# The backward products of a windowed attention in two blocks of four, and one of them in two PSUM tiles

## The chip, the cores and the metric

The kernel runs on one NeuronCore of a Trainium2 chip. The metric is the device time of one execution in microseconds (us), median of several runs. The instructions of the five engines appear here as PE (TensorE matmuls; PEld are its weight loads), ACT (ScalarE), DVE (VectorE), POOL (GpSimd) and SP (SyncE); the last two mainly issue DMAs.

## The reference

The reference computes attention inside 8 x 8 windows of a 256 x 256 picture with 384 channels, in bf16, and all its gradients:

```python
def _fwd_reference(x, wqkv, wo):
    # x: (1, 256, 256, 384) -> xw: (1024 windows, 64 tokens, 384)
    qkv = xw @ wqkv
    q, k, v = qkv[..., :C], qkv[..., C:2 * C], qkv[..., 2 * C:]
    p = softmax(einsum('bqc,bkc->bqk', q, k) * C ** -0.5)
    o = einsum('bqk,bkc->bqc', p, v) @ wo
    return o   # windows put back in their places

def reference(x, wqkv, wo, grad_out):
    out, vjp = jax.vjp(_fwd_reference, x, wqkv, wo)
    return (out, *vjp(grad_out))   # out, dx, dwqkv, dwo
```

## The kernel before, in words

**Tiles.** A tile is two windows, one above the other in the picture: 128 tokens on 128 partitions, the first window on partitions 0 to 63 (`LO`), the second on 64 to 127 (`HI`). Four tiles (`QT`) make a quad, and 128 quads (`NQ`) make the picture. Everything is done quad by quad.

**Weights folded ahead.** Products of weights alone are formed once (`A1_sb`, `A2_sb`, `A3_sb`, `Bm_sb`), so that a quad needs fewer matmuls.

**The front of a quad** prepares it:
- `front_transpose`: DMA transposes, issued on SP, of x and of the output's gradient (`do`) into `xdT`.
- `front_project` (phase "yg"): 18 matmuls of 512 columns with whole 128 x 128 weights, six outputs of three matmuls each, in `ps_yg`; copied to `ygT` in bf16, and transposed by three DMAs into `yg`.
- `front_scores`: the scores of the attention and their counterpart of the gradient into `ps_S`, the one tile of pool `psS` (one PSUM bank).
- `front_softmax`, `front_exp`, `front_ds`: softmax on DVE with one exponential on ACT. They leave `pds`: p and dS.
- `front_zb` (phase "zb"), four times: 6 matmuls of 384 columns, copied by ACT.

**The back of a quad** uses it. `back_transpose` transposes p and dS inside each window on DVE (`pdsT`). Then come products of p, dS or their transposes with 384 columns: W (p with do), U (dS with x), out, and dx (three terms summed in PSUM). Each is formed in two pairs of tiles, p = 0 and p = 1; so there are eight product pairs. In `pair`, each window is a 64 x 64 matmul, and four of them, on the four quarters of the array, start within 0.01 us of each other; the text calls these four a group. W, U and out take one group per pair, dx three. `out` and `dx` are copied to `stage` tiles and stored by three DMAs each on POOL (`back_out`); W and U stay on the chip in `W_sb` and `U_sb` (`back_uw`, L273 to L279).

**Weight gradients.** `weight_grad` (phase "dw") is a generator: each step issues one matmul (128 x 128 weights, 384 columns) that sums x with U or W of the six quads before into `ps_dw`, the one tile of pool `psW`. There are six such chains, and each quad runs one: 24 matmuls from quad 6 on, fewer before. The loop places these matmuls between other work with `fill(chain, n)`. After its last matmul DVE adds `ps_dw` to an accumulator (`G_acc`, `F_acc`; L310, L312).

**Order.** It is written out by hand for PE, ACT, DVE, POOL and SP: every engine works in the order in which the program issues. In an iteration of the main loop (L345 to L374): the do loads of the quad four ahead, the DMA transposes of the quad two ahead, the back's transposes of quad b, the projection of quad b + 1, x loads, then W of both pairs, half of the chain's matmuls, U of both pairs, out of pair 0, the rest of the chain, out of pair 1, dx of both pairs, and the scores and zb phase of quad b + 1.

**PSUM.** Pool `psT` has three tiles of two banks each. ps_yg, ps_W, ps_U, ps_out, ps_dx and ps_zb all take theirs from it in turn, so a product's first matmul waits until the tile that was given out three before it has been copied. `psS` and `psW` have a bank each.

Of the kernel before, what the change touches and what calls it, by code (L numbers as in the profile page):

```python
# [9 lines left out]
ALU = mybir.AluOpType  # L10
AX = mybir.AxisListType
BF16 = mybir.dt.bfloat16
F32 = mybir.dt.float32
ENG = mybir.EngineType

P = 128
# [4 lines left out]
QT = 4  # L21
# [4 lines left out]
def kernel(  # L26
# [11 lines left out]
    nc = tc.nc  # L38
    B, H, W, C = x.shape
# [10 lines left out]
    SPAN = NCH  # L50
# [3 lines left out]
    uwp = ctx.enter_context(tc.tile_pool(name="uwp", bufs=SPAN + 1))  # L54
# [3 lines left out]
    psT = ctx.enter_context(tc.tile_pool(name="psT", bufs=3, space=bass.MemoryType.PSUM))  # L58
    psS = ctx.enter_context(tc.tile_pool(name="psS", bufs=1, space=bass.MemoryType.PSUM))
    psW = ctx.enter_context(tc.tile_pool(name="psW", bufs=1, space=bass.MemoryType.PSUM))  # L60

    mm = nc.tensor.matmul
# [35 lines left out]
    def cut(i):  # L98
        return slice(i * P, (i + 1) * P)
# [9 lines left out]
    def dram(ap, q, t):  # L109
        band, qb = divmod(q, QPB)  # L110
        c0 = (qb * QT + t) * WIN
        return ap[0, band * 2 * WIN:(band + 1) * 2 * WIN, c0:c0 + WIN, :]

    def dram_half(ap, q, t, h):
        band, qb = divmod(q, QPB)
        c0 = (qb * QT + t) * WIN
        r0 = (band * 2 + h) * WIN
        return ap[0, r0:r0 + WIN, c0:c0 + WIN, :]

    st = [dict() for _ in range(NQ)]  # L120
    vec, act = nc.vector.tensor_copy, nc.scalar.copy

    def load_x(q, eng):
        st[q]["x"] = x_tok = tokp.tile([P, QT, C], BF16, name="x_tok")
        for t in range(QT):
            eng.dma_start(out=x_tok[:, t, :], in_=dram(x, q, t))

    def load_do(q):
        st[q]["do"] = do_tok = tokp.tile([P, QT, C], BF16, name="do_tok", bufs=5)
        for t in range(QT):  # L130
            nc.gpsimd.dma_start(out=do_tok[:, t, :], in_=dram(grad_out, q, t))  # L131
# [21 lines left out]
    def swap_halves(q):  # L153
        s = st[q]
        s["xs"] = x_sw = tokp.tile([P, QT // 2, C], BF16, name="x_sw", bufs=SPAN + 1)
        for o, i in ((LO, HI), (HI, LO)):
            nc.vector.tensor_copy(out=x_sw[o], in_=s["x"][i, 1:QT:2, :])
# [3 lines left out]
    def front_project(q):  # L161
        s = st[q]
        s["ygT"] = ygT = quad.tile([P, 2 * CK, QT * P], BF16, name="ygT")
        s["yg"] = yg = quad.tile([P, 2 * CK, QT, P], BF16, name="yg")
        for js, copy in (((0, 1), act), ((2, 3), act), ((4,), act), ((5,), vec)):
            ps = psT.tile([P, 2, QT * P], F32, tag="t", name="ps_yg")
            for i, aj in enumerate(js):
                a, j = divmod(aj, CK)
                A_sb = A3_sb if a else A2_sb
                for m in range(CK):  # L170
                    mm(ps[:, i], lhsT=A_sb[:, m, cut(j)], rhs=s["xdT"][:, a, :, m, :],  # L171
                       start=(m == 0), stop=(m == CK - 1))
            copy(out=ygT[:, js[0]:js[0] + len(js), :], in_=ps[:, 0:len(js)])  # L173
            if js[-1] % 2:
                ks = slice(js[-1] - 1, js[-1] + 1)
                nc.sync.dma_start_transpose(yg[:, ks].rearrange("p j t k -> p (j t) k"),
                                            ygT[:, ks].rearrange("p j k -> p (j k)"))
# [71 lines left out]

    def pair(ps, p, terms):
        t0, t1 = 2 * p, 2 * p + 1
        n = len(terms)
        for k, (lt, rt) in enumerate(terms):
            for o, b, i, t in ((LO, 0, LO, t0), (HI, 0, HI, t0), (HI, 1, LO, t1), (LO, 1, HI, t1)):
                mm(ps[o, b, 0:C], lhsT=lt[i, t, :], rhs=rt(i, t), start=(k == 0), stop=(k == n - 1))  # L257

    def terms_of(q):
        s = st[q]  # L260
        yg = s["yg"]
        p_, ds = s["pds"][:, 0], s["pds"][:, 1]
        pT, dsT = s["pdsT"][:, 0], s["pdsT"][:, 1]
        return {
            "W": [(p_, lambda i, t: s["do"][i, t, :])],
            "U": [(dsT, lambda i, t: s["x"][i, t, :])],
            "out": [(pT, lambda i, t: s["zb"][i, t, 1, :])],
            "dx": [(ds, lambda i, t: yg[i, 0:CK, t, :]),
                   (p_, lambda i, t: yg[i, CK:2 * CK, t, :]),
                   (dsT, lambda i, t: s["zb"][i, t, 0, :])],  # L270
        }

    def back_uw(q, which, p, copy):  # L273
        s = st[q]
        if p == 0:
            s[which] = uwp.tile([P, QT, C], BF16, name=which + "_sb")
        ps = psT.tile([P, 2, 512], F32, tag="t", name="ps_" + which)
        pair(ps, p, terms_of(q)[which])
        copy(out=s[which][:, 2 * p:2 * p + 2, :], in_=ps[:, :, 0:C])  # L279

    def back_out(q, which, p, copy, dst):
        ps = psT.tile([P, 2, 512], F32, tag="t", name="ps_" + which)
        pair(ps, p, terms_of(q)[which])
        o = stage.tile([P, 2, C], BF16, name=which + "_sb")
        copy(out=o[:], in_=ps[:, :, 0:C])  # L285
        nc.gpsimd.dma_start(out=dram(dst, q, 2 * p), in_=o[:, 0, :])  # L286
        nc.gpsimd.dma_start(out=dram_half(dst, q, 2 * p + 1, 1), in_=o[LO, 1, :])  # L287
        nc.gpsimd.dma_start(out=dram_half(dst, q, 2 * p + 1, 0), in_=o[HI, 1, :])  # L288
# [5 lines left out]
    def weight_grad(c, upto, pool, tag):  # L294
        which, acc = (("U", G_acc), ("W", F_acc))[c // CK]
        ma = c % CK
        first = covered[c] == 0
        todo = [(q, t) for q in range(covered[c], upto) for t in range(QT)]
        covered[c] = upto
        if not todo:  # L300
            return
        ps = pool.tile([P, C], F32, tag=tag, name="ps_dw")
        for k, (q, t) in enumerate(todo):
            s = st[q]
            xt = s["xs"][:, t // 2, :] if t % 2 else s["x"][:, t, :]
            mm(ps[:], lhsT=xt[:, cut(ma)], rhs=s[which][:, t, :],  # L306
               start=(k == 0), stop=(k == len(todo) - 1))
            if k == len(todo) - 1:
                if first:
                    nc.vector.tensor_copy(out=acc[:, ma, :], in_=ps[:])  # L310
                else:
                    nc.vector.tensor_tensor(out=acc[:, ma, :], in0=ps[:], in1=acc[:, ma, :], op=ALU.add)  # L312
            yield

    def fill(chain, n):
        for _ in range(n):
            if next(chain, 0) == 0:
                return
# [12 lines left out]
    with tc.manual_schedule(engines={ENG.PE, ENG.Activation, ENG.DVE, ENG.Pool, ENG.SP}):  # L331
        load_x(0, nc.gpsimd)
        load_do(0)
        load_x(1, nc.gpsimd)
        load_do(1)
        front_transpose(0)
        front_transpose(1)
        for q in (2, 3):
            load_x(q, nc.gpsimd)
            load_do(q)  # L340
        front_project(0)
        front_scores(0)
        front_softmax(0)
        zb_phase(0, 1)
        for b in range(NQ):  # L345
            f = b + 1
            ahead = f < NQ
            if b + 4 < NQ:
                load_do(b + 4)
            if b + 2 < NQ:  # L350
                front_transpose(b + 2)
            back_transpose(b)
            if ahead:
                front_project(f)
            if b + 4 < NQ:
                load_x(b + 4, nc.sync)
            chain = weight_grad(b % NCH, b, psW, "w")
            half = 2 * QT * min(b, SPAN) // 4
            back_uw(b, "W", 0, act)
            back_uw(b, "W", 1, vec)  # L360
            swap_halves(b)
            fill(chain, half)
            back_uw(b, "U", 0, act)
            back_uw(b, "U", 1, vec)
            back_out(b, "out", 0, act, out_0)
            for _ in chain:
                pass
            back_out(b, "out", 1, act, out_0)
            back_out(b, "dx", 0, vec, out_1)
            back_out(b, "dx", 1, act, out_1)  # L370
            if ahead:
                front_scores(f)
                front_softmax(f)
                zb_phase(f, f + 1 if f + 1 < NQ else None)  # L374
        for c in sorted(range(NCH), key=lambda c: covered[c]):
            for _ in weight_grad(c, NQ, psT, "t"):
                pass
# [59 lines left out]
```

## Time and profile before

| | |
|---|---|
| median of 3 runs (lowest to highest) | 2013.76 us (2013.29 to 2017.31) |
| the profiled execution, its span | 2016.49 us, 2014.7 us |
| TensorE busy | 1993.8 us (99%), granted clock 0.998 |
| VectorE, ScalarE, GpSimd busy | 69%, 63%, 56% |
| one quad, from quad 6 on | 15.40 us |

The profile is that of one execution. A line of its groups gives line, engine, operation, what is written and read, and the count, then the busy time in us, the mean duration in ns, and the idle time before the instructions with what ended it. A line of the timeline gives start and duration in us, then the instructions; those that follow each other closely are merged (x8), and PEld stands beside PE. A line of the windows gives a stretch, its length, the busy time (and count) of PE, PEld, DVE, ACT and POOL, the granted clock, the DMAs' share and GB/s. Starts of single instructions are given in us from the start of the span; where one quad is followed, the leading 1000 is left out after the first mention (12.362 is 1012.362).

### The profile page before, as it was taken

Reading aid. Unit: us, or ns where it says so; the run is one execution under the profiler, and the core shown is the slowest. Engines: PE = TensorE matmul, PEld = TensorE weight load, DVE = VectorE, ACT = ScalarE, POOL = GpSimd, SP = SyncE. Lnnn points to the kernel's source line nnn. Section 1 sums busy time; section 2 is a strip of 40 time slices with the busy share of each in tenths; the row PEclk is TensorE's granted clock in tenths of the full one; section 3 lists DMA queues with packets and bytes.
Section 4 is the critical chain, followed back from the end, with each engine's and each line's share of the span. In section 5 each row is a group of like instructions: output and inputs, shape, how many; then the busy total and the mean of one; then the engine's idle time right before and its main releaser. Section 6 shows DMA issues by size and latency. Waiting matters only on the chain.

```text
span 2014.7 us, 52710 instructions
## 1 busy us (share of the span) xinstructions
PE 1993.8 (99%) x20862; PEld 1074.6 (53%) x20862; DVE 1394.9 (69%) x2713; ACT 1268.9 (63%) x1689; POOL 1132.0 (56%) x2070
## 2 busy tenths in 40 slices
PE   7999999999999999999999999999999999999998
PEld 4555555555555555555555555555555555555554
DVE  4776677667766776776677667766766776677664
ACT  5666666666666666666666666666666666666663
POOL 5565565555555555655555565555555555555552
PEclk9999999999999999999999999999999999999999
DMA  9999999999999999999999999999999999999982
GB/s 206 213 222 214 208 207 203 202 208 210 196 214 210 199 202 213 210 203 214 199 202 214 193 220 205 199 203 216 207 197 213 206 200 214 207 204 208 206 178 73
DMA packets 979287, 408.89 MB, mean 203 GB/s; under 512 B 864352, under 2 KB 953440, under 8 KB 979040
## 3 DMA queue, kind: packets, MB, share of 16 engines
q1 hardware_dynamic: 879568, 252.26, 75.8%
q0 software_dynamic: 99072, 152.96, 31.2%
q8 instruction: 164, 2.69, 0.6%
q14 instruction: 83, 0.68, 0.1%
q10 hardware_dynamic: 400, 0.29, 0.0%
HBM read 101.84 MB, written 101.84 MB: 101 GB/s over the span
## 4 chain that ended last, share of the span: by engine, by line
PE 97%; DMA 2%; DVE 1%; issue 0%; ACT 0%; SPq 0%; POOL 0%; POOLq 0%
PE ps_dw L306 26%; PE ps_zb L232 25%; PE ps_yg L171 24%; PE ps_dx L257 6%; PE ps_S L187 6%; PE ps_W L257 4%; PE ps_out L257 3%; PE ps_U L257 3%; DMA xdT<-do_tok 1%; DMA yg<-ygT 1%; DMA x_tok<-in_x_dram 0%; PE ps_e L396 0%; ACT dwo_sb L397 0%; DVE ygT L173 0%; DVE pdsT L247 0%
## 5 line engine op out<-in xcount | busy, mean ns | idle before, releaser
L286 POOL DMA_DIRECT2D out_dram<-out_sb x256 | 139.8, 546 | 721.4 <-ACT out_sb L285 715.3
L234 ACT CAST zb<-ps_zb 128x768 bf16<-128x768 f32 x512 | 408.1, 797 | 189.7 <-PE ps_zb L232 171.1
L171 PE MATMUL ps_yg<-xdT,A_sb 128*128 128x512 bf16 x2304 | 518.5, 379 | 0.9 <-DMA xdT<-do_tok 0.9
L232 PEld LDWEIGHTS <-xdT 128*128 128x128 bf16 x3072 | 290.0, 98 | 187.4
L173 ACT CAST ygT<-ps_yg 128x1024 bf16<-128x1024 f32 (+1 forms) x384 | 321.6, 872 | 101.2 <-PE ps_yg L171 100.7
L171 PEld LDWEIGHTS <-A_sb 128*128 128x128 bf16 x2304 | 225.4, 98 | 259.4 <-issue 1.4
L232 PE MATMUL ps_zb<-A_sb,xdT 128*128 128x384 bf16 x1536 | 334.6, 327 | 0.0
L232 PE MATMUL ps_zb<-Bm_sb,xdT 128*128 128x384 bf16 x1536 | 333.3, 326 | 0.0
L285 ACT CAST out_sb<-ps_out 128x768 bf16<-128x768 f32 x256 | 205.1, 802 | 150.5 <-issue 143.3
L131 POOL DMA_DIRECT2D do_tok<-in_grad_out_dram x512 | 272.9, 542 | 33.8 <-issue 16.0
L279 ACT CAST U_sb<-ps_U 128x768 bf16<-128x768 f32 x128 | 102.3, 799 | 238.0 <-PE ps_U L257 238.0
L306 PE MATMUL ps_dw<-U_sb,x_tok 128*128 128x384 bf16 x768 | 251.0, 328 | 0.0
L306 PE MATMUL ps_dw<-W_sb,x_tok 128*128 128x384 bf16 x768 | 251.0, 328 | 0.0
L306 PE MATMUL ps_dw<-W_sb,x_sw 128*128 128x384 bf16 x768 | 249.7, 326 | 0.0
L306 PE MATMUL ps_dw<-U_sb,x_sw 128*128 128x384 bf16 x768 | 249.7, 326 | 0.0
L247 DVE STREAM_TRANSPOSE pdsT<-pds 32x256 bf16<-32x256 bf16 x512 | 223.2, 436 | 12.0
L306 PEld LDWEIGHTS <-x_tok 128*128 128x128 bf16 x1536 | 149.6, 97 | 143.8 <-issue 60.8
L306 PEld LDWEIGHTS <-x_sw 128*128 128x128 bf16 x1536 | 150.4, 98 | 82.8
L279 DVE CAST U_sb<-ps_U 128x768 bf16<-128x768 f32 x128 | 122.6, 958 | 97.3 <-PE ps_U L257 97.0
L209 DVE TENSOR_REDUCE rs<-e 128x4 f32<-128x256 f32 x128 | 53.8, 420 | 171.4 <-ACT e L203 171.4
L288 POOL DMA_DIRECT2D out_dram<-dx_sb x256 | 144.7, 565 | 30.5 <-DMA out_dram<-out_sb 23.9
L287 POOL DMA_DIRECT2D out_dram<-dx_sb x256 | 144.7, 565 | 27.9 <-DMA out_dram<-out_sb 20.2
(71 smaller groups left out, 2606.3 us busy)
## 6 DMA issues: line engine op xcount, KB each, us to landing
do_tok<-in_grad_out_dram POOLq DMA_DIRECT2D x512, 96.0 KB, 5.0
x_tok<-in_x_dram SPq DMA_DIRECT2D x496, 96.0 KB, 4.1
out_dram<-out_sb POOLq DMA_DIRECT2D x256, 96.0 KB, 4.0
out_dram<-out_sb POOLq DMA_DIRECT2D x512, 48.0 KB, 4.2
out_dram<-dx_sb POOLq DMA_DIRECT2D x256, 96.0 KB, 3.6
out_dram<-dx_sb POOLq DMA_DIRECT2D x512, 48.0 KB, 3.7
yg<-ygT SPq DMA_TRANSPOSE x384, 5.2
xdT<-x_tok SPq DMA_TRANSPOSE x128, 5.9
```

Source lines behind the costliest of these rows:

```text
L131: nc.gpsimd.dma_start(out=do_tok[:, t, :], in_=dram(grad_out, q, t))
L171: mm(ps[:, i], lhsT=A_sb[:, m, cut(j)], rhs=s["xdT"][:, a, :, m, :], start=(m == 0), stop=(m == CK - 1))
L173: copy(out=ygT[:, js[0]:js[0] + len(js), :], in_=ps[:, 0:len(js)])
L232: mm(ps[:, i, 0:C], lhsT=s["xdT"][:, 0, t, m, :], rhs=w[:, m, :], start=(m == 0), stop=(m == CK - 1))
L234: nc.scalar.copy(out=s["zb"][:, t], in_=ps[:, :, 0:C])
L247: nc.vector.transpose(out=dst[h + 32 * c:h + 32 * c + 32, :, r, :], in_=src[h + 32 * r:h + 32 * r + 32, :, c, :])
L257: mm(ps[o, b, 0:C], lhsT=lt[i, t, :], rhs=rt(i, t), start=(k == 0), stop=(k == n - 1))
L279: copy(out=s[which][:, 2 * p:2 * p + 2, :], in_=ps[:, :, 0:C])
L285: copy(out=o[:], in_=ps[:, :, 0:C])
L287: nc.gpsimd.dma_start(out=dram_half(dst, q, 2 * p + 1, 1), in_=o[LO, 1, :])
L288: nc.gpsimd.dma_start(out=dram_half(dst, q, 2 * p + 1, 0), in_=o[HI, 1, :])
L306: mm(ps[:], lhsT=xt[:, cut(ma)], rhs=s[which][:, t, :], start=(k == 0), stop=(k == len(todo) - 1))
```

## The change

- The eight product pairs are issued in two blocks, one for each pair: W, U, dx, out. A quarter of the chain's matmuls stand before the first block and the rest before the second. `swap_halves` follows the first block.
- W of a pair takes two PSUM tiles of one bank each in use: its first tile of the pair goes to `ps_We` in pool `psS` (the scores' bank) and is copied by ACT; the second goes to one bank of a `psT` tile and is copied by DVE. Each copy has 384 columns.
- U is copied by ACT in both pairs (before: ACT, DVE), dx by DVE in both (before: DVE, ACT), out by ACT as before.
- The projection's six outputs are copied as 1, 1, 2, 2, all by ACT (before: 2, 2, 1 by ACT and 1 by DVE).
- The accumulation of a chain is issued when the chain is run to its end, which is behind W of the second pair.

```diff
-        for js, copy in (((0, 1), act), ((2, 3), act), ((4,), act), ((5,), vec)):
+        for js, copy in (((0,), act), ((1,), act), ((2, 3), act), ((4, 5), act)):
...
-    def pair(ps, p, terms):
+    def pair(banks, p, terms):
...
-                mm(ps[o, b, 0:C], lhsT=lt[i, t, :], rhs=rt(i, t), start=(k == 0), stop=(k == n - 1))
+                mm(banks[b][o], lhsT=lt[i, t, :], rhs=rt(i, t), start=(k == 0), stop=(k == n - 1))
...
-    def back_uw(q, which, p, copy):
+    def two_banks(name):
+        ps = psT.tile([P, 2, 512], F32, tag="t", name=name)
+        return ps, (ps[:, 0, 0:C], ps[:, 1, 0:C])
+
+    def back_w(q, p):
         s = st[q]
         if p == 0:
-            s[which] = uwp.tile([P, QT, C], BF16, name=which + "_sb")
-        ps = psT.tile([P, 2, 512], F32, tag="t", name="ps_" + which)
-        pair(ps, p, terms_of(q)[which])
-        copy(out=s[which][:, 2 * p:2 * p + 2, :], in_=ps[:, :, 0:C])
+            s["W"] = uwp.tile([P, QT, C], BF16, name="W_sb")
+        one = psS.tile([P, C], F32, tag="s", name="ps_We")
+        _, two = two_banks("ps_W")
+        pair((one[:], two[0]), p, terms_of(q)["W"])
+        act(out=s["W"][:, 2 * p, :], in_=one[:])
+        vec(out=s["W"][:, 2 * p + 1, :], in_=two[0])
+
+    def back_u(q, p):
+        s = st[q]
+        if p == 0:
+            s["U"] = uwp.tile([P, QT, C], BF16, name="U_sb")
+        ps, banks = two_banks("ps_U")
+        pair(banks, p, terms_of(q)["U"])
+        act(out=s["U"][:, 2 * p:2 * p + 2, :], in_=ps[:, :, 0:C])
...
-            half = 2 * QT * min(b, SPAN) // 4
-            back_uw(b, "W", 0, act)
-            back_uw(b, "W", 1, vec)
-            swap_halves(b)
-            fill(chain, half)
-            back_uw(b, "U", 0, act)
-            back_uw(b, "U", 1, vec)
-            back_out(b, "out", 0, act, out_0)
-            for _ in chain:
-                pass
-            back_out(b, "out", 1, act, out_0)
-            back_out(b, "dx", 0, vec, out_1)
-            back_out(b, "dx", 1, act, out_1)
+            left = QT * min(b, SPAN)
+            for p, n in ((0, left // 4), (1, left - left // 4)):
+                fill(chain, n)
+                back_w(b, p)
+                if p == 1:
+                    for _ in chain:
+                        pass
+                back_u(b, p)
+                back_out(b, "dx", p, vec, out_1)
+                back_out(b, "out", p, act, out_0)
+                if p == 0:
+                    swap_halves(b)
```

In `weight_grad` the accumulation moves from the last step of the loop to behind the loop. The numbers of matmuls, of weight loads and of DVE instructions stay as they are; ACT has one copy more a quad.

More of the change, by code (lines that the diff above doesn't have):

```diff
@@ L271, in terms_of @@
         }
-    def back_uw(q, which, p, copy):
+    def two_banks(name):
+        ps = psT.tile([P, 2, 512], F32, tag="t", name=name)
+        return ps, (ps[:, 0, 0:C], ps[:, 1, 0:C])
+    def back_w(q, p):
         s = st[q]
         if p == 0:
-            s[which] = uwp.tile([P, QT, C], BF16, name=which + "_sb")
-        ps = psT.tile([P, 2, 512], F32, tag="t", name="ps_" + which)
-        pair(ps, p, terms_of(q)[which])
-        copy(out=s[which][:, 2 * p:2 * p + 2, :], in_=ps[:, :, 0:C])
+            s["W"] = uwp.tile([P, QT, C], BF16, name="W_sb")
[11 more added lines that the diff above has]
+        act(out=s["U"][:, 2 * p:2 * p + 2, :], in_=ps[:, :, 0:C])
     def back_out(q, which, p, copy, dst):
-        ps = psT.tile([P, 2, 512], F32, tag="t", name="ps_" + which)
-        pair(ps, p, terms_of(q)[which])
+        ps, banks = two_banks("ps_" + which)
+        pair(banks, p, terms_of(q)[which])
         o = stage.tile([P, 2, C], BF16, name=which + "_sb")
@@ L307, in weight_grad @@
                start=(k == 0), stop=(k == len(todo) - 1))
[L308 to L312, printed above, removed]
             yield
+        if first:
+            nc.vector.tensor_copy(out=acc[:, ma, :], in_=ps[:])
+        else:
+            nc.vector.tensor_tensor(out=acc[:, ma, :], in0=ps[:], in1=acc[:, ma, :], op=ALU.add)
     def fill(chain, n):
```

## The prediction

> **What bounds the kernel now.** The page comes first: busy shares, then the chain that ended last.
>
> ```profile
> PE 1993.8 (99%) x20862; PEld 1074.6 (53%) x20862; DVE 1394.9 (69%) x2713; ACT 1268.9 (63%) x1689; POOL 1132.0 (56%) x2070
> ...
> PE 97%; DMA 2%; DVE 1%; issue 0%; ACT 0%; SPq 0%; POOL 0%; POOLq 0%
> ```
>
> TensorE's own order sets the end. But "busy" lasts from a matmul's start to its modelled end (0.33 us for 384 columns, issued every 0.163), so short waits hide inside it. I therefore read starts of single instructions in the trace. The quad period, from one first ps_S matmul to the next, is 15.40 us for all 121 periods from quad 6 on (110.44 to 1974.38 us). One quad in the timeline, first around ps_W:
>
> ```profile
> 1012.39 0.59 ACT L173 CAST ygT<-ps_yg 128x512 bf16<-128x512 f32 x1
> ...
> 1013.04 0.11 PEld L257 LDWEIGHTS <-pds 64*64 64x64 bf16 x3 [0.23 <-issue]
> 1013.08 0.80 ACT L279 CAST W_sb<-ps_W 128x768 bf16<-128x768 f32 x1
> ...
> 1013.32 0.34 PE L306 MATMUL ps_dw<-W_sb,x_tok 128*128 128x384 bf16 x1
> ```
>
> The second W pair waits for a PSUM tile: ACT's 512-column ygT copy ends at 12.983 and the matmul starts at 13.034, 0.362 after the first pair's start, where 0.187 is usual. Then the switches between 64x64 and 128x128 work:
>
> ```profile
> 1014.96 0.33 PE L306 MATMUL ps_dw<-W_sb,x_tok 128*128 128x384 bf16 x1
> 1015.12 0.33 PE L306 MATMUL ps_dw<-W_sb,x_sw 128*128 128x384 bf16 x1
> ...
> 1015.38 0.52 PE L257 MATMUL ps_U<-x_tok,pdsT 64*64 64x384 bf16 x8
> 1015.73 0.33 PE L257 MATMUL ps_out<-zb,pdsT 64*64 64x384 bf16 x4
> ...
> 1015.99 0.34 PE L306 MATMUL ps_dw<-W_sb,x_tok 128*128 128x384 bf16 x1
> ```
>
> ps_dw to ps_dw is 0.163, ps_dw to ps_U 0.256: a switch in costs 0.093, and the first group of four after it 0.024 more (0.187 to the next group, then 0.163). Leaving, ps_out's group to ps_dw is 0.265 and the next spacing 0.172: 0.112. Last, the copies by form:
>
> ```profile
> L173 ACT CAST ygT<-ps_yg 128x1024 bf16<-128x1024 f32 x256 | 259.1, 1012 | 101.2 <-PE ps_yg L171 100.7 <-DMA yg<-ygT 0.5
> ...
> L279 ACT CAST W_sb<-ps_W 128x768 bf16<-128x768 f32 x128 | 102.3, 799 | 12.2
> ...
> L173 ACT CAST ygT<-ps_yg 128x512 bf16<-128x512 f32 x128 | 75.7, 591 | 0.0
> ...
> L279 DVE CAST W_sb<-ps_W 128x768 bf16<-128x768 f32 x128 | 122.6, 958 | 0.0
> ...
> L173 DVE CAST ygT<-ps_yg 128x512 bf16<-128x512 f32 x128 | 88.6, 692 | 30.4 <-PE ps_yg L171 26.7
> ...
> L312 DVE TENSOR_TENSOR F_acc<-ps_dw,F_acc 128x384 f32<-128x384 f32 x63 | 35.1, 558 | 80.9 <-PE ps_dw L306 80.9
> ```
>
> **What it removes, per quad.** From the last ps_yg matmul (12.362) to the first ps_S (19.307) is 6.945 us. Groups and spacings alone make 0.216 + 24 x 0.1625 + 12 x 0.163 = 6.07; the rest, 0.87, is three visits to 64x64 work and the W stall. Gone are one visit (0.093 + 0.024 + 0.112 = 0.229) and the W stall (0.175, and 0.024 because the group after it starts with an empty pipeline: its matmuls last 0.347 and ps_W to ps_dw is 0.289 instead of 0.265). Together 0.43 us: the matmuls that now stand between ps_yg and W are ps_dw, which switches nothing.
>
> **What it adds.** PSUM's three double tiles go round in issue order, so each tile waits for the copy of the third before it. In the new order (W, U, dx, out in each block) out takes W's tile, and waits for DVE's 384-column W copy. That copy has no row: 768 columns take 0.958 and 512 take 0.692 on DVE, so 0.160 + 1.04 ns a column gives 0.559, as the F_acc row of the same width has (0.558). Taken: 0.559; bounds 0.48 (ACT's line through 0.591 and 0.799) and 0.69 (DVE at 512). From W's first start: 0.357 to the end of its fourth matmul, 0.053 to DVE's start (median of the DVE starts after ps_U and ps_dx), 0.559, 0.053 back (six such waits): out may start 1.022 us after W. Without the wait it would start after 0.187 + 0.163 + 3 x 0.163 = 0.838. So 0.184 is lost, and 0.024 after it, twice a quad: 0.42.
>
> [...]
>
> The new walk from 12.362: first ps_dw +0.216; five spacings 0.8125; switch 0.256; W to out 1.022; out to ps_dw 0.289; 17 spacings 0.172 + 2.60; switch 0.256; W to out 1.022; out to ps_S 0.287 (0.263 from ps_dx now, plus 0.024). Sum 6.93 against 6.945: **a gain of 0.013 us a quad, 1.5 us over 121 quads.** Nearly everything gained is handed back to out's wait.
>
> **What costs nothing, and under what cover.** dx waits for the last ygT copy, now 1024 columns on ACT: 12.741 (end of ps_yg) + 0.037 + 1.012 + 0.051 = 13.84; dx comes at 12.362 + 1.285 + 0.350 = 14.00. The cover is 0.16 us; beyond it, another 0.18 goes into out's wait before the quad is longer. U waits for the ygT copy that ends at 12.50, and for pdsT, ready at 12.62, against 13.83. The short first ps_yg tiles ask for zb's copies sooner: the third, at 9.99, needs the zb copy that ends at 9.69. ps_S waits for ACT's copy of W's second half: 0.41 + 0.48 + 0.05 after W, where ps_S comes 1.31 after. On DVE the accumulation and dx's copy now stand between W's copy and nmx, which moves 0.1 us later; exp is held by the zb copy on ACT anyway (its end is 0.7 us behind e_in's). The first block's dx and out stores reach POOL's queue about 2 us earlier (dx's copy ends at 15.7, the first store stands at 17.58 now), and the do loads queued behind the stores move up as much; SP's queue is busy 13.1 of 15.4 us (8.89 to 22.01) and keeps its order. yg's transposes land 4.3 us after ps_S at the latest of four quads read past the start (1562.8 for 1558.5), and dx needs them 10.1 after. If that cover went, dx and all behind it would wait.
>
> **The edges.** In quads 0 to 5 there is less ps_dw to lie before W, and SP is a lap behind: yg lands at 35.16 (quad 0) and 79.25 (quad 3), and dx stands waiting. Before, only the rest of dx follows that wait; now also out, ps_dw, W, U and the second dx and out. The same walk gives +1.15 us (quad 0), -0.3, +0.2, and +2.3 at quad 3: nine ps_dw and four groups, the first of them in a stretch at half clock as now:
>
> ```profile
> 79.00:82.40 3.40, 3.10 (x68) 2.23 (x67) 0.96 (x1) 0.80 (x1) 2.07 (x5) 0.50 1.17 286
> ```
>
> (the 0.50 is the granted clock). Quad 4 gives -0.5 (its project phase ran partly in that stretch): +2.9 in all, 0 to +6. In the last quad U waits for pdsT until 1983.16 and has six ps_dw fewer before it: +0.6. Edges: **+3.5 us**.
>
> **Sum:** -1.5 + 3.5 = +2.0 on an execution of 2016.49 us (span 2014.7, 1.8 outside it, 2.7 over the median). On the median of 2013.76: **2015.8 us**. A measurement of this kernel tells some 0.2%, 4 us, from no change, so most of this case is "same". Its own range: the copy's duration and its two hand-overs within 0.02 (2 x 0.02 x 121 = 5 us), the edges 3 either way: 2010 to 2022.
>
> **The rivals.**
> 1. *Out hardly waits* (faster). If W's half is copied in 0.48, ACT's pace, each wait shrinks by 0.08: 19 us, 1996; by half of that, 2006; with no wait at all, 0.42 x 121 = 51 us, 1965. For it: two engines share the copy, and DVE has been idle since 12.62. Against: two DVE rows and the accumulation row agree on 0.56. [...]
> 2. *dx waits for ACT* (slower). The 1024-column ygT copy is now ACT's last of the phase. It decides from 0.34 us of lateness on (0.16 + 0.18). If ACT ran one 512-column copy late (0.483 as they issue), the quad grows by 0.14, 17 us: 2033. For: ACT now copies all of ps_yg. Against: its queue stands idle before that copy (the 101.2 us of waits for ps_yg in the row above). Chance 0.12.
> 3. *Every group pays for its wait* (slower). Each of the eight now begins with a wait; if the six that are met in time also emptied the pipeline, 6 x 0.024 x 121 = 17 us: 2033. For: after the W stall the group paid it. Against: dx's first group waits for three semaphores today and its spacing is the 0.163 of others. Chance 0.10.
> 4. *The change does not do what it says*: the switches fall by one visit only if ps_yg and ps_dw need none between them; ps_zb to ps_yg today is 0.163, no switch. If it had one, 0.2 x 121 = 24 us more, 2040. Chance 0.02.
>
> **Chances and range.** Forecast 0.63, rivals 0.13, 0.12, 0.10, 0.02. Within the forecast some 0.66 is "same", 0.27 slower (centre +2.0, bound +4, spread 5), 0.07 faster. Faster: 0.13 + 0.04 = 0.17. Slower: 0.24 + 0.17 = 0.41. Same: 0.42. Eight in ten: the forecast's range widened to half of rival 1 and most of rivals 2 and 3, 2006 to 2031.
>
> **What would show it.** In the new profile: quad period 15.39; ps_yg to ps_dw 0.216; W's DVE copy 0.56, and 1.02 us from W's first start to out's, with "DVE W_sb" as releaser; ps_out group to ps_dw 0.289; no wait of dx for ygT; early S starts some 3 us late by quad 5. If out starts 0.84 after W, rival 1 is right; if dx waits for ACT, rival 2; if groups are 0.187 apart throughout, rival 3.

## The result and the profile after

| | before | after |
|---|---|---|
| median of 5 runs each (lowest to highest), us | 2015.62 (2013.29 to 2017.31) | 2023.52 (2023.0 to 2029.22) |
| profiled execution's span, us | 2014.7 | 2027.4 |
| one quad, from ps_S to ps_S, median, us | 15.405 | 15.443 |
| ninth ps_S (us from the start) | 141.25 | 145.56 |
| last ps_S to the end, us | 40.3 | 44.2 |

The ratio is 1.0046 (95% interval 1.003 to 1.0062): slower by 0.46%, some 8 us, more than the 0.2% by which the runs of the kernel before differ (2013.29 to 2017.31). Of the table's differences, 0.038 us in each of 119 quads make 4.5 us; the rest lies at the two ends. The profiled execution of the changed kernel is the slowest of the five, so the ends weigh more in it than in the median.

The page of the profile after, busy shares and the chain:

```profile
PE 1992.8 (98%) x20862; PEld 1110.5 (55%) x20862; DVE 1306.9 (64%) x2713; ACT 1331.7 (66%) x1945; POOL 1134.0 (56%) x2070
...
PE 96%; DMA 2%; issue 1%; DVE 1%; ACT 0%; POOL 0%; DVEq 0%; ACTq 0%; SPq 0%; POOLq 0%
```

ACT has 1945 instructions for 1689, two more a quad and not the one that the section on the change counts: the projection, W and U add one each, dx takes one away. TensorE still carries the chain; as before, its share of busy time hides what costs. The first block of one quad in the timeline (start, duration, instructions; weight loads and others left out):

```profile
958.06 0.33 PE L322 MATMUL ps_dw<-U_sb,x_sw 128*128 128x384 bf16 x1
...
958.32 0.35 PE L257 MATMUL ps_We<-do_tok,pds 64*64 64x384 bf16 x2
958.32 0.35 PE L257 MATMUL ps_W<-do_tok,pds 64*64 64x384 bf16 x2
...
958.50 0.33 PE L257 MATMUL ps_U<-x_tok,pdsT 64*64 64x384 bf16 x4
...
958.66 0.49 PE L257 MATMUL ps_dx<-yg,pds 64*64 64x384 bf16 x8
958.71 0.48 ACT L286 CAST W_sb<-ps_We 128x384 bf16<-128x384 f32 x1 [0.25 <-PE ps_W L257]
958.75 0.56 DVE L287 CAST W_sb<-ps_W 128x384 bf16<-128x384 f32 x1 [1.46 <-PE ps_W L257]
...
958.99 0.33 PE L257 MATMUL ps_dx<-zb,pdsT 64*64 64x384 bf16 x4
...
959.36 0.36 PE L257 MATMUL ps_out<-zb,pdsT 64*64 64x384 bf16 x4
959.36 0.11 PEld L257 LDWEIGHTS <-pdsT 64*64 64x64 bf16 x3 [0.27 <-issue]
```

W, U and the three groups of dx follow each other at 0.163 to 0.187: no switch, and W waits for nothing. Then out, which would follow dx's third group (958.99) at 959.15, starts at 959.36, 0.05 after DVE's copy of W ends at 959.31. Three of its weight loads stand behind its first matmul, as they did at the W stall before. Note the two copies of W: ACT starts at 958.706, DVE at 958.749. The copies by form:

```profile
L287 DVE CAST W_sb<-ps_W 128x384 bf16<-128x384 f32 x256 | 142.7, 558 | 434.2 <-PE ps_W L257 434.1
...
L173 ACT CAST ygT<-ps_yg 128x1024 bf16<-128x1024 f32 x256 | 259.1, 1012 | 127.1 <-PE ps_yg L171 127.1
...
L286 ACT CAST W_sb<-ps_We 128x384 bf16<-128x384 f32 x256 | 122.5, 478 | 338.3 <-PE ps_W L257 338.1
```

DVE's copy is 0.558 and ACT's 0.478. The list of waits has out waiting for DVE's copy only twice, 0.7 us in all, since dx's last matmuls last until almost the moment that out starts (958.99 + 0.33); the wait is read from the starts.

### The profile page after: what moved, and what is told of

It is laid out like the page before. It is cut to its first block, busy times and chain, and to the rows that moved or that the text cites. A ratio compares the mean times of both kernels' runs of the same rounds, so it can differ in the third digit from the quotient of the medians.

```text
span 2027.4 us, 52829 instructions
## 1 busy us (share of the span) xinstructions
PE 1992.8 (98%) x20862; PEld 1110.5 (55%) x20862; DVE 1306.9 (64%) x2713; ACT 1331.7 (66%) x1945; POOL 1134.0 (56%) x2070
## 4 chain that ended last, share of the span: by engine, by line
PE 96%; DMA 2%; issue 1%; DVE 1%; ACT 0%; POOL 0%; DVEq 0%; ACTq 0%; SPq 0%; POOLq 0%
PE ps_dw L322 25%; PE ps_zb L232 25%; PE ps_yg L171 24%; PE ps_dx L257 6%; PE ps_S L187 5%; PE ps_out L257 4%; PE ps_We L257 3%; PE ps_U L257 2%; DMA yg<-ygT 1%; DMA xdT<-do_tok 0%; PE ps_c L95 0%; PE ps_e L410 0%; DMA do_tok<-in_grad_out_dram 0%; DMA w_sb<-in_wqkv_dram 0%; DMA out_dram<-out_sb 0%
## 5 line engine op out<-in xcount | busy, mean ns | idle before, releaser
L302 POOL DMA_DIRECT2D out_dram<-dx_sb x256 | 144.3, 564 | 783.5 <-DVE dx_sb L301 781.8
L173 ACT CAST ygT<-ps_yg 128x512 bf16<-128x512 f32 (+1 forms) x512 | 409.7, 800 | 128.3 <-PE ps_yg L171 127.2
L287 DVE CAST W_sb<-ps_W 128x384 bf16<-128x384 f32 x256 | 142.7, 558 | 434.2 <-PE ps_W L257 434.1
L286 ACT CAST W_sb<-ps_We 128x384 bf16<-128x384 f32 x256 | 122.5, 478 | 338.3 <-PE ps_W L257 338.1
L301 DVE CAST dx_sb<-ps_dx 128x768 bf16<-128x768 f32 x256 | 243.9, 953 | 20.5 <-PE ps_dx L257 11.5
L295 ACT CAST U_sb<-ps_U 128x768 bf16<-128x768 f32 x256 | 206.1, 805 | 2.7 <-PE ps_U L257 2.6
L257 PEld LDWEIGHTS <-pdsT 64*64 64x64 bf16 x3072 | 115.8, 106 | 93.4 <-issue 67.6
```

The costliest lines, as they stand in the source:

```text
L257: mm(banks[b][o], lhsT=lt[i, t, :], rhs=rt(i, t), start=(k == 0), stop=(k == n - 1))
L287: vec(out=s["W"][:, 2 * p + 1, :], in_=two[0])
L295: act(out=s["U"][:, 2 * p:2 * p + 2, :], in_=ps[:, :, 0:C])
```

## The experiments

Periods are medians over the quads from the eleventh on, "W to out" is the median from the first start of W's group to out's. Every ratio is to runs of the kernel before on the same chip as the run (median 2014.20 us for the first four, 2015.22 for the last).

### The change once more (after_again)

The same kernel.

> The changed kernel once more, beside the next three. Theory: from quad 8 on the period is 15.44 us again, since out starts 1.048 us after W in every quad; what differs from execution to execution lies in the first eight quads and in the last (yg's transposes landing late, stretches at half clock). Expected time 2020 to 2030, period 15.44. Rival: the 0.037 us a quad came of that one execution; then the period is another one.

Measured: 2023.54 us, 1.0042 times the kernel before (1.0027 to 1.0056); period 15.442 (15.443 in the first), W to out 1.046 (1.047). In its profiled execution the ninth ps_S came at 141.24, as in the kernel before, and the span was 2021.8. So the 0.038 us a quad is the kernel's, and what the start costs changes with the execution: in the first profile quad 6 stood 1.84 us for yg's transposes, and TensorE then ran 3.4 us at half clock; here it didn't. Those lines of the first profile:

```profile
121.29 0.33 PE L257 MATMUL ps_dx<-yg,pds 64*64 64x384 bf16 x4
123.46 0.36 PE L257 MATMUL ps_dx<-yg,pds 64*64 64x384 bf16 x4 [1.84 <-DMA yg<-ygT]
```

and the stretch after them, in the view of windows (busy PE, PEld, DVE, ACT, POOL, then the granted clock):

```profile
124.70:128.10 3.40, 3.40 (x13) 1.64 (x11) 0.99 (x3) 0.33 (x1) 2.82 (x6) 0.50 1.31 157
```

### The psT half first (first_half)

```diff
-        pair((one[:], two[0]), p, terms_of(q)["W"])
-        act(out=s["W"][:, 2 * p, :], in_=one[:])
-        vec(out=s["W"][:, 2 * p + 1, :], in_=two[0])
+        pair((two[0], one[:]), p, terms_of(q)["W"])
+        vec(out=s["W"][:, 2 * p, :], in_=two[0])
+        act(out=s["W"][:, 2 * p + 1, :], in_=one[:])
```

> W's halves change places: the psT half is the one that the first two matmuls of the group fill, still copied by DVE; the scores' bank takes the other two, copied by ACT. Theory A (TensorE's two completions are signalled one after the other: the first reaches its engine 0.035 us after the matmul's end, the second 0.077): DVE starts 0.035 after the end, out starts 0.350 + 0.035 + 0.558 + 0.055 = 0.998 after W instead of 1.048, so 0.10 less a quad: period 15.34, 12 us less. Rival B (DVE is late because ACT starts a PSUM copy at the same moment): the hand-over stays 0.077, out starts 1.040 after W, period 15.42, 2 us less.

Measured: 2013.1 us, 0.9995 of the kernel before (0.9986 to 1.0005), so level with it; period 15.355, W to out 1.003. The timeline:

```profile
903.26 0.35 PE L257 MATMUL ps_W<-do_tok,pds 64*64 64x384 bf16 x2
903.27 0.35 PE L257 MATMUL ps_We<-do_tok,pds 64*64 64x384 bf16 x2
...
903.65 0.56 DVE L286 CAST W_sb<-ps_W 128x384 bf16<-128x384 f32 x1 [1.42 <-PE ps_We L257]
903.69 0.48 ACT L287 CAST W_sb<-ps_We 128x384 bf16<-128x384 f32 x1 [0.29 <-PE ps_We L257]
...
904.26 0.36 PE L257 MATMUL ps_out<-zb,pdsT 64*64 64x384 bf16 x4
```

Now DVE starts first (903.654) and ACT 0.040 later (903.694). The two still start within 0.04 of each other, and DVE is no longer late, so rival B falls; the copy of the half that TensorE finishes first starts first. The gain was 0.087 a quad, not 0.10: the 0.035 had been taken from the end of the group's last matmul, and the expectation added it to the end of its second, 0.007 earlier.

### The engines exchanged (act_half)

```diff
-        act(out=s["W"][:, 2 * p, :], in_=one[:])
-        vec(out=s["W"][:, 2 * p + 1, :], in_=two[0])
+        vec(out=s["W"][:, 2 * p, :], in_=one[:])
+        act(out=s["W"][:, 2 * p + 1, :], in_=two[0])
```

> The engines change places: ACT copies the psT half (the group's last two matmuls), DVE the half in the scores' bank. ACT's 384-column copy took 0.478 where DVE's took 0.558. Theory A (second signal 0.077 after the end, whichever engine waits): out starts 0.357 + 0.077 + 0.478 + 0.051 = 0.963 after W, 0.085 less twice a quad: period 15.27, 21 us less. Rival B (ACT is reached in 0.035 wherever it stands): 0.921, period 15.19, 31 us less. If out's wait were not what sets the quad, the period stays 15.44.

Measured: 2006.46 us, 0.9956 (0.9939 to 0.9972); period 15.277, W to out 0.963, theory A's figures. The timeline:

```profile
917.46 0.35 PE L257 MATMUL ps_We<-do_tok,pds 64*64 64x384 bf16 x2
...
917.86 0.56 DVE L286 CAST W_sb<-ps_We 128x384 bf16<-128x384 f32 x1 [1.42 <-PE ps_W L257]
917.90 0.48 ACT L287 CAST W_sb<-ps_W 128x384 bf16<-128x384 f32 x1 [0.29 <-PE ps_W L257]
...
918.43 0.36 PE L257 MATMUL ps_out<-zb,pdsT 64*64 64x384 bf16 x4
```

ACT, now second, starts 0.434 after W, where it starts 0.392 after W in the changed kernel. For the moment at which these copies start, the engine doesn't matter, its place does.

### Both together (first_act)

```diff
-        pair((one[:], two[0]), p, terms_of(q)["W"])
-        act(out=s["W"][:, 2 * p, :], in_=one[:])
-        vec(out=s["W"][:, 2 * p + 1, :], in_=two[0])
+        pair((two[0], one[:]), p, terms_of(q)["W"])
+        act(out=s["W"][:, 2 * p, :], in_=two[0])
+        vec(out=s["W"][:, 2 * p + 1, :], in_=one[:])
```

> Both together: the psT half comes of the first two matmuls and is copied by ACT, the scores' half of the last two by DVE. Out starts 0.350 + 0.035 + 0.478 + 0.051 = 0.914 after W, 0.134 less twice a quad: period 15.17, 33 us less, some 1991, below the kernel before. The next wait would be ps_S for DVE's copy of the scores' half: 0.357 + 0.077 + 0.558 + 0.055 = 1.05 after W, where ps_S then comes at 1.20; if that hand-over is slower than 0.23, the gain is smaller.

Measured: 1995.51 us, 0.9903 of the kernel before (0.9888 to 0.9918): faster by 1.0%. Period 15.190, W to out 0.921 (0.392 + 0.478 + 0.051); 15.17 and 0.914 were expected, again with the 0.035 added to the second matmul's end. Past the first quads ps_S does not wait for DVE's copy:

```profile
900.35 0.48 ACT L286 CAST W_sb<-ps_W 128x384 bf16<-128x384 f32 x1 [2.35 <-PE ps_We L257]
900.39 0.56 DVE L287 CAST W_sb<-ps_We 128x384 bf16<-128x384 f32 x1 [1.90 <-PE ps_We L257]
...
900.88 0.36 PE L257 MATMUL ps_out<-zb,pdsT 64*64 64x384 bf16 x4
901.16 0.63 PE L187 MATMUL ps_S<-xdT,ygT 128*64 128x64 bf16 x27
```

DVE's copy ends at 900.95, and ps_S starts at 901.16, 0.28 after out.

### Two thirds of the copy taken away (part_copy)

```diff
-        vec(out=s["W"][:, 2 * p + 1, :], in_=two[0])
+        vec(out=s["W"][:, 2 * p + 1, 0:P], in_=two[0][:, 0:P])
+        vec(out=s["W"][:, 2 * p + 1, P:C], in_=s["x"][:, 2 * p + 1, P:C])
```

> The changed kernel, but DVE copies only 128 of 384 columns out of the psT half of W; the other 256 columns of W_sb are filled from x in SBUF, so W's weight gradient is not computed rightly. Theory: nothing is left to wait for (0.357 + 0.077 + 0.293 + 0.055 = 0.78 after W, where out comes by itself at 0.838), so each out loses its wait of 0.21 and the 0.024 of the empty pipeline: period 15.442 - 2 x 0.233 = 14.98, time some 1967. Rival: another wait stands right behind (ps_S for ACT's copy at 0.91 after W, or dx for ygT), and the period falls by less.

This kernel leaves out part of what W's gradient needs and serves to measure alone. Measured: 1967.93 us in one run, period 14.974, W to out 0.837. Nothing else stands behind out's wait:

```profile
900.17 0.29 DVE L287 CAST W_sb<-ps_W 128x128 bf16<-128x128 f32 x1 [1.46 <-PE ps_W L257]
900.41 0.33 PE L257 MATMUL ps_dx<-zb,pdsT 64*64 64x384 bf16 x4
...
900.58 0.33 PE L257 MATMUL ps_out<-zb,pdsT 64*64 64x384 bf16 x4
```

So the wait costs 15.442 - 14.974 = 0.468 us a quad in the changed kernel, where the expectation has 2 x 0.233, and what the change takes away is worth 15.405 - 14.974 = 0.43, the prediction's figure. Of out's wait, "both together" keeps 15.190 - 14.974 = 0.22 us a quad.

### W whole, in the two blocks (whole_w)

```diff
-        one = psS.tile([P, C], F32, tag="s", name="ps_We")
-        _, two = two_banks("ps_W")
-        pair((one[:], two[0]), p, terms_of(q)["W"])
-        act(out=s["W"][:, 2 * p, :], in_=one[:])
-        vec(out=s["W"][:, 2 * p + 1, :], in_=two[0])
+        ps, banks = two_banks("ps_W")
+        pair(banks, p, terms_of(q)["W"])
+        act(out=s["W"][:, 2 * p:2 * p + 2, :], in_=ps[:, :, 0:C])
```

> The two blocks without W's split: W of a pair in one psT tile, copied by ACT with 768 columns (0.799). Theory: out starts 0.357 + 0.05 + 0.799 + 0.05 = 1.26 after W instead of 1.047, period 15.44 + 2 x 0.21 = 15.86, time some 2075: the order alone loses, and the split is what brings it back to even. Rival: W's place in the scores' bank or its second engine has a cost of its own; then the period is under 15.86.

Measured: 2076.98 us in one run, period 15.867, W to out 1.259. Here the wait is long enough for the list of waits to show it, 248 times:

```profile
PE ps_out L257 <- ACT W_sb L285: 62.5, 248, 0.3
```

and one quad of its timeline:

```profile
899.23 0.36 PE L257 MATMUL ps_W<-do_tok,pds 64*64 64x384 bf16 x4
...
899.64 0.80 ACT L285 CAST W_sb<-ps_W 128x768 bf16<-128x768 f32 x1 [0.27 <-PE ps_W L257]
...
900.49 0.36 PE L257 MATMUL ps_out<-zb,pdsT 64*64 64x384 bf16 x4 [0.25 <-ACT W_sb L285]
```

With one copy instead of two, it starts 0.408 after W (median), where the prediction's terms give 0.357 + 0.053 = 0.410. The order of blocks alone would cost 0.46 us a quad; the split earns back 0.42 of it.

### The projection's copies as before (old_proj)

```diff
-        for js, copy in (((0,), act), ((1,), act), ((2, 3), act), ((4, 5), act)):
+        for js, copy in (((0, 1), act), ((2, 3), act), ((4,), act), ((5,), vec)):
```

> The changed kernel with the projection's copies as before (2, 2, 1 by ACT, 1 by DVE). Theory: the projection's copies are all done before their tiles are asked for, in either form: period 15.44 as with the change, within 0.01. Rival: the last ygT copy holds dx in one of the two forms; then the period differs by what it is late.

Measured: 2023.39 us in one run, period 15.443, W to out 1.047. This part of the change weighs nothing here.

### The old order at the edges (edges)

The kernel of "both together", and in the main loop (`back_whole` is the former `back_uw`, W or U of a pair in one psT tile):

```diff
-            for p, n in ((0, left // 4), (1, left - left // 4)):
+            if b <= SPAN or not ahead:
+                back_whole(b, "W", 0, act)
+                back_whole(b, "W", 1, vec)
...
+                back_out(b, "dx", 1, act, out_1)
+            for p, n in () if b <= SPAN or not ahead else ((0, left // 4), (1, left - left // 4)):
```

> The version with W's psT half first and copied by ACT (1995.5 us), and in quads 0 to 6 and the last one the order of the kernel before, with W whole. Theory: the blocks cost at the edges, where yg lands late or pdsT is awaited: the ninth ps_S near 141.3 in every execution, the stretch from the last ps_S to the end 40.3 instead of 44.5, period 15.19 unchanged: some 1990. Rival: the edges are TensorE's clock steps and fall where they will; then the time stays near 1995.

Measured: 1990.21 us, 0.9878 of the kernel before on the same chip (0.9855 to 0.9902). This is the lowest median of all versions that compute the whole, faster than both kernels by 1.2% and more. Period 15.193, unchanged; the ninth ps_S came at 136.44 (141.67 without this edit), 4.8 before that of the kernel before, and the stretch from the last ps_S to the end took 42.0 (44.5 without). Expected were 141.3 and 40.3. The 1.7 that the end is longer than 40.3 goes with a stretch at a granted clock of 0.50 (1954.62 to 1958.03), which the kernel before doesn't have there; most of the start's 4.8 is quad 3, which took 13.43 where it took 17.37 in the kernel before, and the order doesn't explain it, being the old one there. The profiled spans differ by 7.4 us (1986.4 and 1993.8), but each is one execution, and the intervals of the two ratios overlap; the gain over "both together" is not shown by the times.

## Why the prediction was right in its range and off by 6 us

The range, 2006 to 2031, held the time, and the gain was handed back to out's wait as the prediction said, with some 0.04 us a quad on top: 0.47 lost against 0.43 gained. The centre was 2.0 us slower, the measurement 7.9; "same" had a chance of 0.42 and "slower", which came, 0.41.

- **What it removes: right.** 0.43 us a quad, as the kernel in which out doesn't wait shows. ps_yg to ps_dw was 0.216, so rival 4 is out.
- **The copy: right.** 0.558 (mean of 256 copies; the shortest took 0.556), where 0.559 was taken from two other widths (0.692 at 512 columns, 0.958 at 768); so rival 1 is out.
- **The hand-over to DVE: mis-sized.** The term "0.053 to DVE's start" came from ps_U and ps_dx, where one signal leaves the group. The change splits W over two engines, so two signals leave it, and DVE, which waits for the second, starts 0.077 after the group's end. Out starts 1.047 after W instead of 1.022. Twice in 121 quads that is 6 us, the whole difference between 2.0 and 7.9, and the period is 15.442 where 15.391 was forecast.
- **What costs nothing: right.** dx waits for no ygT copy past the first quads; the projection's form changes nothing; U, ps_S and zb wait for none of the new copies. Rivals 2 and 3 did not come about: groups that found their tile free were 0.163 apart.
- **The edges: right in size, by luck, and wrong in the pieces.** 7.9 measured less 4.5 of the quads leaves 3.4, where 3.5 stood. But the walk put 2.3 us on quad 3; in both profiles of the changed kernel that quad was 3.7 us shorter than before (13.62 for 17.37), quad 0 was 1.7 and 3.9 longer, and the end 2.6 and 3.9 longer where 0.6 was forecast. The seventh ps_S, forecast some 3 late, was 0.09 early in one of them and 0.75 late in the other. In the shorter of the two profiles the end's own part is 0.95 (the last gradients' start) and the rest a stretch at a granted clock of 0.51 (2010.50 to 2013.90) that falls into the last products. When yg lands in the first quads, and why quad 3 no longer waits, is not settled by these runs: in all nine profiles other than that of the kernel before, "the old order at the edges" included, it took 13.4 to 14.9 us, and the kernel before has one profile only, so the 17.37 may be that execution's.

The mechanism of the mis-sized term was shown by moving it: the start of W's copies after W's own start, medians.

| kernel | signalled first | second | alone |
|---|---|---|---|
| after | ACT 0.392 | DVE 0.434 | |
| first_half | DVE 0.393 | ACT 0.434 | |
| act_half | DVE 0.393 | ACT 0.434 | |
| first_act | ACT 0.392 | DVE 0.436 | |
| whole_w | | | ACT 0.408 |

The place decides: not the engine, and not which of the two tiles is copied. The traces hold the signals themselves, as events of the semaphore that the copies wait for (medians). Where two are sent, the group's second matmul sends one at 0.369 after W's start and the fourth the other at 0.412 (0.368 and 0.411 in the first profile); where one is sent, in whole_w, the fourth sends it at 0.386. Each copy starts 0.022 to 0.024 behind its signal, so the delay arises before an engine starts to copy.

The last signal comes 0.026 later with another before it (0.412) than alone (0.386), and the first 0.017 sooner than a lone one (0.369): that is the 0.043 between the two. The second matmul starts 0.007 before the fourth; the other 0.010, and what holds the last signal up by 0.026, no run explains.

## What to carry to other kernels

When an order change saves switches on the bound engine, walk the tile rotation of the new order: the third-before tile's copy may now end last, and its time from write to release (end, signal, copy, signal back) has to fit under the work between (here what did not fit cost 0.468 us a quad). Where a group of matmuls feeds two readers, let the tile that is wanted back first be the one signalled first, and give it to the engine with the shorter copy (384 columns took 0.478 on ACT, 0.558 on DVE): here that turned 0.4% slower into 1.0% faster without touching the order. Price a hand-over from a row with as many signals as the new code will send: here 0.053 was read behind one signal, and the second of two took 0.077.

## What the runs showed that was not expected

- Two signals of one group of four matmuls leave some 0.043 us apart, so the copies that wait for them start 0.392 and 0.434 after the group's start, and one that waits for a lone signal at 0.408.
- Near the start and the end TensorE stood for up to 3.3 us at a time (dx's longest wait for yg's transposes, in the first profile of the changed kernel). Every profile has 3.4 or 6.8 us at a granted clock of 0.50 in its first 45 us, and all but that of the kernel before again 3.4 us or more behind the last ps_S, at other places in each and not behind every stand: the edges differ by up to 5.6 us between two profiled executions of the same kernel (spans 2027.4 and 2021.8) while the period agrees to 0.001.
